# One 128-row DMA per output tile in place of two 64-row DMAs

## Chip, cores and metric

One core of one Trainium2 chip. The metric is the device time of one execution in microseconds (us); medians of several runs are given. A ratio is the mean time of one kernel's runs over that of the other's from the same rounds, so it is not quite the ratio of the medians quoted.

## The reference, cut to what matters

A decayed linear attention in blocks of 64 tokens (4 batches, 8 heads, 768 tokens, head size 64), and then an MLP on its 3072 x 512 output. Only the last line writes memory: 3072 rows of 512 fp32, 6.29 MB.

```python
intra = einsum(einsum(qb, kb) * Dmask, vb)
inter = einsum(qb * lam_pow, kv_state)          # kv_state is carried from block to block
x = attn_out.transpose(0, 2, 1, 3).reshape(B * S, H * D)
h = x @ w_in
g = h + sin(alpha * h) ** 2 / (alpha + 1e-09)
return g @ w_out                                 # [3072, 512] fp32
```

## The kernel before

The work is a list, `ORDER`, of small steps with the engine for each; every engine runs its own steps in the order of the list. Six row groups `g` of 512 tokens have four output tiles `m` of 128 rows each. Unit `u` is a quarter of a row group's attention: loads of q, k, v (`ld`), two DMA transposes (`tdq`, `tdk`), scores on TensorE (`s`), their mask on VectorE (`m`). SyncE (`S`) issues all loads, transposes and stores (`st.g.m.par`).

```python
outp = ctx.enter_context(tc.tile_pool(name="outp", bufs=4))     # four output buffers
# ...
def out_rows(g, m):
    _, tp, b, _, _ = where(4 * g + 2 * (m // 2))
    r0 = b * S + tp * W + (m % 2) * C
    return out[r0:r0 + C].rearrange("(p two) d -> two p d", two=2)

def out_copy(g, m, eng, **_):
    obs[g, m] = outp.tile([P, DM], FP32, name="ob")
    copy(eng, obs[g, m][:], ops.pop((g, m))[:])                 # PSUM to SBUF

def store(g, m, par, **_):
    nc.sync.dma_start(out=out_rows(g, m)[par], in_=obs[g, m][par * D:(par + 1) * D, :])
```

The loads bring two neighbouring tokens to one partition, so the even rows of an output tile lie in partitions 0 to 63 and the odd rows in 64 to 127. That is why the store has a `par` for parity, and why each of its two DMAs writes every second row. The last tile is stored in column pieces by other code, which the change does not touch.

Of the kernel before, what the change touches and what calls it, by code (L numbers as in the profile page):

```python
# [625 lines left out]
```

## Time and profile before

| | |
|---|---|
| median time | 215.98 us when predicted; 216.06 with a fourth run |
| span in the profile | 213.8 us |
| TensorE busy | 204.0 us, 95% |
| DMA engines busy | about 100% up to some 128 us, little after |
| stores of 64 rows | 46, each 64 packets of 2 KB; 20 of them from 185 us on |

The prediction shows the lines. One more is the page's packet count of the kernel before; "under 512 B" counts the 256 B packets of the transposes and the small completion records (4 B) that a DMA leaves.

```profile
DMA packets 64009, 33.92 MB, mean 159 GB/s; under 512 B 19680, under 2 KB 61040, under 8 KB 63984
```

### The profile page before, as it was taken

The numbers are of one execution on the slowest core, as the hardware profiler recorded it, in microseconds if no ns is written. First come the engines' busy times: TensorE is split into PE (matmuls) and PEld (weight loads), VectorE is DVE, ScalarE is ACT, GpSimd is POOL, SyncE is SP. The second block draws the span as 40 slices with busy tenths as digits, with TensorE's granted clock in tenths as the row PEclk, the third lists the DMA queues.
The fourth block names the chain that finished last, engine by engine and source line by source line (L and its number), as shares of the span: only waits on it lengthen the run. The fifth ranks groups of instructions, "written<-read, shape, count | busy, mean of one in ns | idle before, by whom it ended". The sixth has DMA issues, their size and how long they took to land.

```text
span 213.8 us, 5465 instructions
## 1 busy us (share of the span) xinstructions
PE 204.0 (95%) x2104; PEld 110.1 (51%) x2132; DVE 129.8 (61%) x235; ACT 123.5 (58%) x244; POOL 141.4 (66%) x208
## 2 busy tenths in 40 slices
PE   7989999999999999999799999999999999999993
PEld 5767544457744554455444554454454444444463
DVE  3885798159599845778667785626884626441120
ACT  3563984077899839986394496936635659131001
POOL 5488389689797999999898996709841728030000
PEclk9999999999999999999999999999999999999999
DMA  5999999999999999989899997520610000171624
GB/s 144 293 235 196 187 204 271 282 291 289 200 205 202 248 213 289 208 103 199 218 268 133 223 179 198 92 49 0 132 44 3 0 0 0 35 179 35 147 51 98
DMA packets 64009, 33.92 MB, mean 159 GB/s; under 512 B 19680, under 2 KB 61040, under 8 KB 63984
## 3 DMA queue, kind: packets, MB, share of 16 engines
q1 hardware_dynamic: 59568, 29.31, 62.5%
q0 software_dynamic: 4224, 4.19, 12.4%
...
q10 hardware_dynamic: 192, 0.07, 0.2%
q14 instruction: 9, 0.07, 0.1%
HBM read 27.28 MB, written 6.29 MB: 157 GB/s over the span
## 4 chain that ended last, share of the span: by engine, by line
PE 67%; POOL 12%; DMA 10%; issue 3%; ACT 2%; SPq 2%; DVE 2%; POOLq 0%; ACTq 0%
PE ops L525 27%; PE hps L482 24%; DMA w_out_sb<-in_moe_w_out_dram 4%; PE bz L564 3%; DMA QT<-KD 2%; PE okv L460 2%; POOL KD L300 2%; POOL kvbd L425 2%; PE sp L368 2%; PE bz L588 2%; DMA st_v<-in_v_dram 2%; POOL QL L300 2%; POOL kvx L421 2%; PE pt L327 2%; SPq L259 2%
## 5 line engine op out<-in xcount | busy, mean ns | idle before, releaser
L482 PE MATMUL hps<-xt,w_in_sb 128*128 128x512 bf16 (+1 forms) x404 | 86.4, 362 | 0.6 <-issue 0.2
L525 PE MATMUL ops<-w_out_sb,gall 128*128 128x512 bf16 x352 | 83.2, 379 | 2.1 <-issue 1.3
L516 DVE SCALAR_TENSOR_TENSOR gall<-s,r_sb,hps 128x512 bf16<-128x512 bf16 x96 | 68.3, 744 | 23.3 <-POOL s L511 11.7
L502 ACT ACTIVATE s<-hps,alpha_sb 128x512 bf16<-128x512 f32 x96 | 63.2, 688 | 25.7 <-PE hps L482 25.1
L482 PEld LDWEIGHTS <-w_in_sb 128*128 128x128 bf16 x416 | 39.8, 98 | 40.6
L511 POOL TENSOR_TENSOR s<-s 128x512 bf16<-128x512 bf16 x35 | 36.3, 1045 | 36.3 <-ACT s L502 35.6
L525 PEld LDWEIGHTS <-gall 128*128 128x128 bf16 x368 | 34.6, 98 | 39.9 <-issue 0.6
L378 DVE TENSOR_TENSOR ST<-sp,mask 128x512 bf16<-128x512 f32 x48 | 31.9, 684 | 4.4 <-PE sp L368 4.2
L509 ACT ACTIVATE s<-s 128x512 bf16<-128x512 bf16 x51 | 31.6, 634 | 1.0 <-DVE gall L516 0.4
L284 DVE COPY ob<-ops 128x512 f32<-128x512 f32 (+1 forms) x13 | 8.6, 659 | 29.2 <-PE ops L525 23.6
L300 POOL TENSOR_TENSOR QL<-st_q,E 128x512 bf16<-128x512 f32 x23 | 23.9, 1042 | 3.6 <-DVE alpha_sb L574 2.2
L300 POOL TENSOR_TENSOR KD<-st_k,R 128x512 bf16<-128x512 f32 x22 | 22.9, 1042 | 3.5 <-DMA st_k<-in_k_dram 1.8
L425 POOL TENSOR_TENSOR kvbd<-kvx,LBD 128x256 bf16<-128x256 f32 x32 | 19.6, 612 | 2.5
L282 ACT COPY ob<-ops 128x512 f32<-128x512 f32 (+2 forms) x13 | 7.1, 547 | 22.4 <-PE ops L550 12.0
L282 ACT CAST xt<-okv 128x256 bf16<-128x256 f32 x29 | 9.8, 374 | 11.8 <-PE okv L460 11.8
L421 POOL TENSOR_TENSOR kvx<-kva,kvs 128x128 f32<-128x128 f32 x32 | 14.7, 460 | 1.2 <-ACT kva L282 1.0
L284 DVE CAST xt<-okv 128x256 bf16<-128x256 f32 x19 | 7.7, 420 | 11.5 <-PE okv L460 11.5
L282 ACT COPY kva<-kvp 128x128 f32<-128x128 f32 x26 | 6.4, 273 | 9.9 <-PE kvp L400 8.9
L368 PE MATMUL sp<-QT 64*64 64x128 bf16 x384 | 9.9, 219 | 1.3 <-DMA QT<-KD 1.3
L282 ACT COPY QT<-pt 128x512 bf16<-128x512 bf16 x9 | 5.2, 591 | 9.8 <-PE pt L327 9.7
L460 PE MATMUL okv<-ST,VB 64*64 64x128 bf16 x384 | 9.9, 220 | 0.0
L282 ACT CAST VB<-st_v 128x512 bf16<-128x512 f32 x14 | 8.6, 625 | 1.9 <-DMA st_v<-in_v_dram 1.8
...
## 6 DMA issues: line engine op xcount, KB each, us to landing
...
QT<-QL SPq DMA_TRANSPOSE x16, 4.1
QT<-KD SPq DMA_TRANSPOSE x16, 3.4
```

The source lines that it names most:

```text
L282: nc.scalar.copy(out=out, in_=in_)
L284: eng.tensor_copy(out=out, in_=in_)
L300: eng.tensor_tensor(out=t[:], in0=stage[u, j][:].rearrange("p h two e -> p two h e"), in1=tab[:, :, hh * HH:(hh + 1) * HH].unsqueeze(3).to ...
L378: nc.vector.tensor_tensor(out=stm[u][:, hd], in0=sps[u][hd][:], in1=mask[:].unsqueeze(2).to_broadcast([P, 2, 2, P]), op=ALU.mult)
L421: eng.tensor_tensor(out=t[:], in0=x, in1=prev[:], op=ALU.add)
L425: eng.tensor_tensor(out=kvbd[u, c][:], in0=x.unsqueeze(2).to_broadcast([P, 2, 2, D]), in1=LBD[:, 2 * hh:2 * hh + 2, :].unsqueeze(3).to_bro ...
L482: f1mm[g, f] = nc.tensor.matmul(out=hps[g, f][:].rearrange("p (b i) -> p b i", b=2)[:, bs] .rearrange("p b i -> p (b i)"), lhsT=w_in_sb[:, ...
L502: nc.scalar.activation(out=s1[g, f][:], in_=hps[g, f][:], func=ACTF.Sin, scale=alpha_sb[:, f:f + 1])
L509: nc.scalar.activation(out=s2[g, f][:], in_=x[:], func=ACTF.Square)
L511: eng.tensor_tensor(out=s2[g, f][:], in0=x[:], in1=x[:], op=ALU.mult)
L516: nc.vector.scalar_tensor_tensor(out=gall[g][:, f, :], in0=s2.pop((g, f))[:], scalar=r_sb[:, f:f + 1], in1=hps.pop((g, f))[:], op0=ALU.mul ...
L525: nc.tensor.matmul(out=ops[g, m][:], lhsT=gall[g][:, f, m * P:(m + 1) * P], rhs=w_out_sb[:, f, :], start=(f == 0), stop=(f == NFC - 1))
```

## The change

Its intent: half as many store issues on SyncE, and transfers of 256 KB from all 128 partitions in place of 128 KB from 64. In the order, the second store of each tile is dropped and the first stays where it was (most of the diff's other lines are the list wrapped anew).

```diff
-tdq.9:S s.8:T a.8.0:G sk.10:G st.0.0.0:S ld.12.0:S tdk.9:S st.0.0.1:S stt.1.6:V stt.1.7:V sin.1.8:A
+tdq.9:S s.8:T a.8.0:G sk.10:G st.0.0.0:S ld.12.0:S tdk.9:S stt.1.6:V stt.1.7:V sin.1.8:A sqr.1.8:A
 ... (22 more such stores dropped)
-    def store(g, m, par, **_):
-        nc.sync.dma_start(out=out_rows(g, m)[par], in_=obs[g, m][par * D:(par + 1) * D, :])
+    def store(g, m, _i, **_):
+        nc.sync.dma_start(out=out_rows(g, m), in_=obs[g, m][:])
```

More of the change, by code (lines that the diff above doesn't have):

```diff
@@ L51 @@
 sin.1.6:A stt.1.4:V stt.1.5:V sin.1.7:A f1.1.9:T:2 kc.9.0:V sqr.1.6:A f1.1.10:T:7 kc.9.1:A sqr.1.7:A
-tdq.9:S s.8:T a.8.0:G sk.10:G st.0.0.0:S ld.12.0:S tdk.9:S st.0.0.1:S stt.1.6:V stt.1.7:V sin.1.8:A
-sqr.1.8:A sin.1.9:A sin.1.10:A stt.1.8:V m.8.0:V f1.1.11:T:3 f1.1.12:T:0 f1.1.13:T:1 sq.11:G
-tdq.10:S sin.1.11:A f1.1.14:T:4 ld.12.1:S ld.12.2:S ld.13.0:S sqr.1.9:V sqr.1.10:A sqr.1.11:G
-stt.1.9:V stt.1.10:V sin.1.12:A sqr.1.12:G sin.1.13:A stt.1.11:V stt.1.12:V m.8.1:V sk.11:G
-f1.1.15:T:2 cv.10:G sin.1.14:A sqr.1.13:A oi.8:T sin.1.15:A tdk.10:S f2.1.0.0:T:3 sqr.1.14:A sk.12:G
@@ L57 @@
-sq.12:G f2.1.0.1:T f2.1.0.2:T a.9.0:G sqr.1.15:A cv.11:A stt.1.13:V stt.1.14:V stt.1.15:V s.9:T
-o.8:T tdq.11:S ld.13.1:S ld.13.2:S k.10:T:0,1 x.8.0:A x.8.1:A m.9.0:V tdk.11:S f2.1.0.3:T m.9.1:V
-oi.9:T kc.10.0:A st.0.1.0:S ld.14.0:S kc.10.1:A o.9:T cv.12:A x.9.0:A s.10:T k.11:T:2,0 f2.1.1.0:T:1
+tdq.9:S s.8:T a.8.0:G sk.10:G st.0.0.0:S ld.12.0:S tdk.9:S stt.1.6:V stt.1.7:V sin.1.8:A sqr.1.8:A
+sin.1.9:A sin.1.10:A stt.1.8:V m.8.0:V f1.1.11:T:3 f1.1.12:T:0 f1.1.13:T:1 sq.11:G tdq.10:S
+sin.1.11:A f1.1.14:T:4 ld.12.1:S ld.12.2:S ld.13.0:S sqr.1.9:V sqr.1.10:A sqr.1.11:G stt.1.9:V
@@ L60 @@
+stt.1.10:V sin.1.12:A sqr.1.12:G sin.1.13:A stt.1.11:V stt.1.12:V m.8.1:V sk.11:G f1.1.15:T:2
+cv.10:G sin.1.14:A sqr.1.13:A oi.8:T sin.1.15:A tdk.10:S f2.1.0.0:T:3 sqr.1.14:A sk.12:G sq.12:G
+f2.1.0.1:T f2.1.0.2:T a.9.0:G sqr.1.15:A cv.11:A stt.1.13:V stt.1.14:V stt.1.15:V s.9:T o.8:T
+tdq.11:S ld.13.1:S ld.13.2:S k.10:T:0,1 x.8.0:A x.8.1:A m.9.0:V tdk.11:S f2.1.0.3:T m.9.1:V oi.9:T
+kc.10.0:A st.0.1.0:S ld.14.0:S kc.10.1:A o.9:T cv.12:A x.9.0:A s.10:T k.11:T:2,0 f2.1.1.0:T:1
 m.10.0:V a.10.0:G x.9.1:A kc.11.0:A kc.11.1:A m.10.1:V oi.10:T k.12:T:2,0 n.6.0:G n.8.0:G n.9.0:G
@@ L61 @@
 s.11:T o.10:T kc.12.0:V f2.1.1.1:T ld.14.1:S m.11.0:V ld.14.2:S n.10.0:G x.10.0:V m.11.1:V
-f2.1.1.2:T ld.15.0:S st.0.1.1:S ld.15.1:S tdq.12:S ld.15.2:S ld.16.0:S ld.16.1:S ld.16.2:S ld.17.0:S
-oc.1.0:A kc.12.1:A x.10.1:A a.11.0:G sk.13:G cv.13:G oi.11:T o.11:T x.11.0:A sq.13:G f2.1.1.3:T
-sq.14:G oc.1.1:A n.7.0:G x.11.1:V f1.2.0:T:6 sin.2.0:A f1.2.1:T:5 sin.2.1:A sqr.2.0:A stt.2.0:V
-ld.17.1:S st.1.1.0:S a.6.1:G n.6.1:G sk.14:G ld.17.2:S st.0.3.0:S st.0.2.0:S f1.2.2:T:2 sin.2.2:A
-sqr.2.1:A stt.2.1:V f1.2.3:T:7 sin.2.3:A f1.2.4:T:0 f1.2.5:T:3 sin.2.4:A f1.2.6:T:4 f1.2.7:T:5
@@ L67 @@
-sqr.2.2:G stt.2.2:V sqr.2.3:A a.5.1:G stt.2.3:V sin.2.5:A f1.2.8:T:6 f1.2.9:T:7 f1.2.10:T:1 sq.15:G
-sk.15:G sqr.2.4:A sin.2.6:A sqr.2.5:A stt.2.4:V f2.1.2.0:T:0 stt.2.5:V cv.14:G f1.2.11:T:3 tdk.12:S
-f1.2.12:T:2 sin.2.7:A f2.1.2.1:T st.0.2.1:S sin.2.8:A sqr.2.6:G sqr.2.7:A stt.2.6:V sin.2.9:A
-stt.2.7:V sqr.2.8:G sin.2.10:A n.11.0:G stt.2.8:V sqr.2.9:A sqr.2.10:A stt.2.9:V stt.2.10:V sq.16:G
-sin.2.11:A sqr.2.11:A tdq.13:S n.5.1:G tdk.13:S tdq.14:S st.0.3.1:S tdk.14:S a.7.1:G a.12.0:G s.12:T
@@ L72 @@
-k.13:T:6,7 kc.13.0:A sin.2.12:A kc.13.1:A sqr.2.12:A m.12.0:V m.12.1:V tdq.15:S f1.2.13:T:1
-f2.1.2.2:T sin.2.13:A sqr.2.13:A oi.12:T s.13:T o.12:T stt.2.11:V f2.1.2.3:T a.13.0:G m.13.0:V
-stt.2.12:V m.13.1:V stt.2.13:V x.12.0:A x.12.1:A f2.1.3.0:T:3 n.13.0:G n.7.1:G a.8.1:G oi.13:T
-sk.16:G oc.1.2:A f1.2.14:T:2 o.13:T k.14:T:1,0 s.14:T sin.2.14:A x.13.0:V x.13.1:V m.14.0:V n.8.1:G
-sq.17:G n.12.0:G kc.14.0:A f2.1.3.1:T m.14.1:V f2.1.3.2:T sqr.2.14:A a.14.0:G kc.14.1:A tdk.15:S
-ld.18.0:S ld.18.1:S oi.14:T ld.18.2:S sq.18:G cv.15:A cv.16:G cv.17:A k.15:T:1,0 o.14:T s.15:T
@@ L78 @@
-tdq.16:S tdk.16:S stt.2.14:V kc.15.0:V x.14.0:V x.14.1:A f1.2.15:T:2 f2.1.3.3:T st.1.2.0:S a.15.0:G
-m.15.0:V kc.15.1:V oi.15:T m.15.1:V ld.19.0:S ld.19.1:S ld.19.2:S s.16:T ld.20.0:S st.1.0.0:S o.15:T
-x.15.0:V k.16:T:1 x.15.1:V sin.2.15:A sqr.2.15:A m.16.0:V oc.1.3:V stt.2.15:V a.11.1:G f2.2.0.0:T:0
-f1.3.0:T:7 kc.16.0:A st.1.0.1:S ld.20.1:S m.16.1:V sin.3.0:A sqr.3.0:A f1.3.1:T:4 f1.3.2:T:6
-sin.3.1:A f1.3.3:T:1 sqr.3.1:A sin.3.2:A sin.3.3:A f1.3.4:T:5 sin.3.4:A f1.3.5:T:2 f1.3.6:T:3
-sk.17:G st.1.2.1:S ld.20.2:S sk.18:G sk.19:G f2.2.0.1:T f2.2.0.2:T a.9.1:G sq.19:G sq.20:G sqr.3.2:G
@@ L84 @@
-stt.3.0:V sqr.3.3:A stt.3.1:V a.16.0:G n.9.1:G sin.3.5:A sqr.3.4:A stt.3.2:V n.14.0:G n.15.0:G
-sin.3.6:A stt.3.3:V stt.3.4:V sqr.3.5:A ld.21.0:S tdq.17:S tdk.17:S sqr.3.6:A cv.18:G tdq.18:S
-tdk.18:S st.1.3.0:S f1.3.7:T:1 oi.16:T stt.3.5:V a.10.1:G s.17:T o.16:T x.16.0:V k.17:T:2 f2.2.0.3:T
-cv.19:G m.17.0:V stt.3.6:V x.16.1:V kc.17.0:A f2.2.1.0:T:2 a.17.0:G n.10.1:G n.11.1:G sk.20:G
-cv.20:G a.12.1:G f2.2.1.1:T tdq.19:S ld.21.1:S tdk.19:S ld.21.2:S ld.22.0:S st.1.1.1:S tdq.20:S
-ld.22.1:S tdk.20:S m.17.1:V oi.17:T oc.2.0:V s.18:T st.1.3.1:S k.18:T:3 k.19:T:0 o.17:T kc.18.0:A
@@ L90 @@
-f2.2.1.2:T a.18.0:G sin.3.7:A x.17.0:A x.17.1:A n.12.1:G f2.2.1.3:T m.18.0:V m.18.1:V f1.3.8:T:3
-oi.18:T oc.2.1:V sqr.3.7:A sin.3.8:A sqr.3.8:A sq.21:G ld.22.2:S ld.23.0:S st.2.1.0:S sk.21:G
-kc.19.0:V s.19:T o.18:T k.20:T:2 kc.20.0:A m.19.0:V stt.3.7:V f1.3.9:T:0 m.19.1:V f1.3.10:T:4
-sin.3.9:A stt.3.8:V a.19.0:G f1.3.11:T:1 st.2.0.0:S x.18.0:A x.18.1:V sqr.3.9:G sk.22:G sin.3.10:A
-sqr.3.10:A f1.3.12:T:3 f1.3.13:T:2 oi.19:T stt.3.9:V sin.3.11:A sqr.3.11:A sin.3.12:A stt.3.10:V
-cv.21:A f2.2.2.0:T:0 f2.2.2.1:T f2.2.2.2:T stt.3.11:V a.20.0:G sqr.3.12:A sin.3.13:A o.19:T s.20:T
@@ L96 @@
-f1.3.14:T:1 x.19.0:A sqr.3.13:G sq.22:G x.19.1:V sin.3.14:A m.20.0:V stt.3.12:V f1.3.15:T:6
-f1.4.0:T:7 sqr.3.14:G stt.3.13:V stt.3.14:V sin.3.15:A sin.4.0:A sqr.3.15:A sqr.4.0:A stt.3.15:V
-stt.4.0:V tdq.21:S st.2.0.1:S ld.23.1:S f2.2.2.3:T oc.2.2:A f1.4.1:T:4 a.13.1:G cv.22:G sin.4.1:A
-sqr.4.1:G m.20.1:V f1.4.2:T:3 f1.4.3:T:0 sin.4.2:A sin.4.3:A sqr.4.2:A sqr.4.3:A sq.23:G
-f2.2.3.0:T:1 f2.2.3.1:T tdk.21:S tdq.22:S ld.23.2:S oi.20:T n.13.1:G f2.2.3.2:T f2.2.3.3:T o.20:T
-k.21:T:2 stt.4.1:V s.21:T stt.4.2:V stt.4.3:V kc.21.0:V oc.2.3:A f2.3.0.0:T:0 f1.4.4:T:3 f2.3.0.1:T
@@ L102 @@
-f1.4.5:T:2 x.20.0:A sin.4.4:A sin.4.5:A sqr.4.4:G a.15.1:G sqr.4.5:G stt.4.4:V m.21.0:V m.21.1:V
-stt.4.5:V f1.4.6:T:1 sin.4.6:A tdk.22:S tdq.23:S sqr.4.6:A stt.4.6:V a.21.0:G st.2.3.0:S f2.3.0.2:T
-f1.4.7:T:6 f1.4.8:T:3 f2.3.0.3:T sk.23:G oc.3.0:V f1.4.9:T:1 f1.4.10:T:5 f1.4.11:T:4 x.20.1:V
-sin.4.7:A sin.4.8:A sqr.4.7:G sqr.4.8:G stt.4.7:V stt.4.8:V cv.23:A f1.4.12:T:2 tdk.23:S st.3.0.0:S
-sin.4.9:A sqr.4.9:A stt.4.9:V sin.4.10:A sqr.4.10:G stt.4.10:V f2.3.1.0:T:3 f2.3.1.1:T n.15.1:G
-sin.4.11:A st.2.2.0:S st.2.1.1:S sqr.4.11:A stt.4.11:V oi.21:T o.21:T k.22:T:0 k.23:T:1 s.22:T
@@ L108 @@
-x.21.0:V m.22.0:V x.21.1:V m.22.1:V f2.3.1.2:T f2.3.1.3:T oc.3.1:V st.2.3.1:S a.14.1:G n.14.1:G
-kc.22.0:A a.22.0:G oi.22:T o.22:T s.23:T m.23.0:V f2.3.2.0:T:0 f2.3.2.1:T x.22.0:V kc.23.0:A
-x.22.1:A m.23.1:V a.23.0:G oi.23:T f2.3.2.2:T f1.4.13:T:3 o.23:T x.23.0:V f1.4.14:T:4 x.23.1:V
-f1.4.15:T:1 sin.4.12:A sqr.4.12:A stt.4.12:V sin.4.13:A st.2.2.1:S st.3.0.1:S sin.4.14:A sqr.4.13:A
+f2.1.1.2:T ld.15.0:S ld.15.1:S tdq.12:S ld.15.2:S ld.16.0:S ld.16.1:S ld.16.2:S ld.17.0:S oc.1.0:A
+kc.12.1:A x.10.1:A a.11.0:G sk.13:G cv.13:G oi.11:T o.11:T x.11.0:A sq.13:G f2.1.1.3:T sq.14:G
@@ new lines @@
+oc.1.1:A n.7.0:G x.11.1:V f1.2.0:T:6 sin.2.0:A f1.2.1:T:5 sin.2.1:A sqr.2.0:A stt.2.0:V ld.17.1:S
+st.1.1.0:S a.6.1:G n.6.1:G sk.14:G ld.17.2:S st.0.3.0:S st.0.2.0:S f1.2.2:T:2 sin.2.2:A sqr.2.1:A
+stt.2.1:V f1.2.3:T:7 sin.2.3:A f1.2.4:T:0 f1.2.5:T:3 sin.2.4:A f1.2.6:T:4 f1.2.7:T:5 sqr.2.2:G
+stt.2.2:V sqr.2.3:A a.5.1:G stt.2.3:V sin.2.5:A f1.2.8:T:6 f1.2.9:T:7 f1.2.10:T:1 sq.15:G sk.15:G
+sqr.2.4:A sin.2.6:A sqr.2.5:A stt.2.4:V f2.1.2.0:T:0 stt.2.5:V cv.14:G f1.2.11:T:3 tdk.12:S
+f1.2.12:T:2 sin.2.7:A f2.1.2.1:T sin.2.8:A sqr.2.6:G sqr.2.7:A stt.2.6:V sin.2.9:A stt.2.7:V
@@ new lines @@
+sqr.2.8:G sin.2.10:A n.11.0:G stt.2.8:V sqr.2.9:A sqr.2.10:A stt.2.9:V stt.2.10:V sq.16:G sin.2.11:A
+sqr.2.11:A tdq.13:S n.5.1:G tdk.13:S tdq.14:S tdk.14:S a.7.1:G a.12.0:G s.12:T k.13:T:6,7 kc.13.0:A
+sin.2.12:A kc.13.1:A sqr.2.12:A m.12.0:V m.12.1:V tdq.15:S f1.2.13:T:1 f2.1.2.2:T sin.2.13:A
+sqr.2.13:A oi.12:T s.13:T o.12:T stt.2.11:V f2.1.2.3:T a.13.0:G m.13.0:V stt.2.12:V m.13.1:V
+stt.2.13:V x.12.0:A x.12.1:A f2.1.3.0:T:3 n.13.0:G n.7.1:G a.8.1:G oi.13:T sk.16:G oc.1.2:A
+f1.2.14:T:2 o.13:T k.14:T:1,0 s.14:T sin.2.14:A x.13.0:V x.13.1:V m.14.0:V n.8.1:G sq.17:G n.12.0:G
@@ new lines @@
+kc.14.0:A f2.1.3.1:T m.14.1:V f2.1.3.2:T sqr.2.14:A a.14.0:G kc.14.1:A tdk.15:S ld.18.0:S ld.18.1:S
+oi.14:T ld.18.2:S sq.18:G cv.15:A cv.16:G cv.17:A k.15:T:1,0 o.14:T s.15:T tdq.16:S tdk.16:S
+stt.2.14:V kc.15.0:V x.14.0:V x.14.1:A f1.2.15:T:2 f2.1.3.3:T st.1.2.0:S a.15.0:G m.15.0:V kc.15.1:V
+oi.15:T m.15.1:V ld.19.0:S ld.19.1:S ld.19.2:S s.16:T ld.20.0:S st.1.0.0:S o.15:T x.15.0:V k.16:T:1
+x.15.1:V sin.2.15:A sqr.2.15:A m.16.0:V oc.1.3:V stt.2.15:V a.11.1:G f2.2.0.0:T:0 f1.3.0:T:7
+kc.16.0:A ld.20.1:S m.16.1:V sin.3.0:A sqr.3.0:A f1.3.1:T:4 f1.3.2:T:6 sin.3.1:A f1.3.3:T:1
@@ new lines @@
+sqr.3.1:A sin.3.2:A sin.3.3:A f1.3.4:T:5 sin.3.4:A f1.3.5:T:2 f1.3.6:T:3 sk.17:G ld.20.2:S sk.18:G
+sk.19:G f2.2.0.1:T f2.2.0.2:T a.9.1:G sq.19:G sq.20:G sqr.3.2:G stt.3.0:V sqr.3.3:A stt.3.1:V
+a.16.0:G n.9.1:G sin.3.5:A sqr.3.4:A stt.3.2:V n.14.0:G n.15.0:G sin.3.6:A stt.3.3:V stt.3.4:V
+sqr.3.5:A ld.21.0:S tdq.17:S tdk.17:S sqr.3.6:A cv.18:G tdq.18:S tdk.18:S st.1.3.0:S f1.3.7:T:1
+oi.16:T stt.3.5:V a.10.1:G s.17:T o.16:T x.16.0:V k.17:T:2 f2.2.0.3:T cv.19:G m.17.0:V stt.3.6:V
+x.16.1:V kc.17.0:A f2.2.1.0:T:2 a.17.0:G n.10.1:G n.11.1:G sk.20:G cv.20:G a.12.1:G f2.2.1.1:T
@@ new lines @@
+tdq.19:S ld.21.1:S tdk.19:S ld.21.2:S ld.22.0:S tdq.20:S ld.22.1:S tdk.20:S m.17.1:V oi.17:T
+oc.2.0:V s.18:T k.18:T:3 k.19:T:0 o.17:T kc.18.0:A f2.2.1.2:T a.18.0:G sin.3.7:A x.17.0:A x.17.1:A
+n.12.1:G f2.2.1.3:T m.18.0:V m.18.1:V f1.3.8:T:3 oi.18:T oc.2.1:V sqr.3.7:A sin.3.8:A sqr.3.8:A
+sq.21:G ld.22.2:S ld.23.0:S st.2.1.0:S sk.21:G kc.19.0:V s.19:T o.18:T k.20:T:2 kc.20.0:A m.19.0:V
+stt.3.7:V f1.3.9:T:0 m.19.1:V f1.3.10:T:4 sin.3.9:A stt.3.8:V a.19.0:G f1.3.11:T:1 st.2.0.0:S
+x.18.0:A x.18.1:V sqr.3.9:G sk.22:G sin.3.10:A sqr.3.10:A f1.3.12:T:3 f1.3.13:T:2 oi.19:T stt.3.9:V
@@ new lines @@
+sin.3.11:A sqr.3.11:A sin.3.12:A stt.3.10:V cv.21:A f2.2.2.0:T:0 f2.2.2.1:T f2.2.2.2:T stt.3.11:V
+a.20.0:G sqr.3.12:A sin.3.13:A o.19:T s.20:T f1.3.14:T:1 x.19.0:A sqr.3.13:G sq.22:G x.19.1:V
+sin.3.14:A m.20.0:V stt.3.12:V f1.3.15:T:6 f1.4.0:T:7 sqr.3.14:G stt.3.13:V stt.3.14:V sin.3.15:A
+sin.4.0:A sqr.3.15:A sqr.4.0:A stt.3.15:V stt.4.0:V tdq.21:S ld.23.1:S f2.2.2.3:T oc.2.2:A
+f1.4.1:T:4 a.13.1:G cv.22:G sin.4.1:A sqr.4.1:G m.20.1:V f1.4.2:T:3 f1.4.3:T:0 sin.4.2:A sin.4.3:A
+sqr.4.2:A sqr.4.3:A sq.23:G f2.2.3.0:T:1 f2.2.3.1:T tdk.21:S tdq.22:S ld.23.2:S oi.20:T n.13.1:G
@@ new lines @@
+f2.2.3.2:T f2.2.3.3:T o.20:T k.21:T:2 stt.4.1:V s.21:T stt.4.2:V stt.4.3:V kc.21.0:V oc.2.3:A
+f2.3.0.0:T:0 f1.4.4:T:3 f2.3.0.1:T f1.4.5:T:2 x.20.0:A sin.4.4:A sin.4.5:A sqr.4.4:G a.15.1:G
+sqr.4.5:G stt.4.4:V m.21.0:V m.21.1:V stt.4.5:V f1.4.6:T:1 sin.4.6:A tdk.22:S tdq.23:S sqr.4.6:A
+stt.4.6:V a.21.0:G st.2.3.0:S f2.3.0.2:T f1.4.7:T:6 f1.4.8:T:3 f2.3.0.3:T sk.23:G oc.3.0:V
+f1.4.9:T:1 f1.4.10:T:5 f1.4.11:T:4 x.20.1:V sin.4.7:A sin.4.8:A sqr.4.7:G sqr.4.8:G stt.4.7:V
+stt.4.8:V cv.23:A f1.4.12:T:2 tdk.23:S st.3.0.0:S sin.4.9:A sqr.4.9:A stt.4.9:V sin.4.10:A
@@ L112 @@
+sqr.4.10:G stt.4.10:V f2.3.1.0:T:3 f2.3.1.1:T n.15.1:G sin.4.11:A st.2.2.0:S sqr.4.11:A stt.4.11:V
+oi.21:T o.21:T k.22:T:0 k.23:T:1 s.22:T x.21.0:V m.22.0:V x.21.1:V m.22.1:V f2.3.1.2:T f2.3.1.3:T
+oc.3.1:V a.14.1:G n.14.1:G kc.22.0:A a.22.0:G oi.22:T o.22:T s.23:T m.23.0:V f2.3.2.0:T:0 f2.3.2.1:T
+x.22.0:V kc.23.0:A x.22.1:A m.23.1:V a.23.0:G oi.23:T f2.3.2.2:T f1.4.13:T:3 o.23:T x.23.0:V
+f1.4.14:T:4 x.23.1:V f1.4.15:T:1 sin.4.12:A sqr.4.12:A stt.4.12:V sin.4.13:A sin.4.14:A sqr.4.13:A
 sqr.4.14:G stt.4.13:V stt.4.14:V f1.5.0:T:5 f1.5.1:T:7 sin.4.15:A sqr.4.15:A sin.5.0:A sin.5.1:A
@@ L119 @@
 f2.4.1.0:T:3 f2.4.1.1:T f2.4.1.2:T oc.4.0:V f1.5.14:T:1 sqr.5.10:G stt.5.10:V sqr.5.11:G sqr.5.12:A
-stt.5.11:V stt.5.12:V st.4.0.0:S st.3.2.0:S st.3.2.1:S st.3.3.0:S st.3.1.0:S st.3.3.1:S f1.5.15:T:7
-sin.5.13:A sin.5.14:A st.3.1.1:S f2.4.1.3:T oc.4.1:V sqr.5.13:A sqr.5.14:G sin.5.15:A stt.5.13:V
-stt.5.14:V f2.4.2.0:T:4 st.4.0.1:S st.4.1.0:S st.4.1.1:S sqr.5.15:G stt.5.15:V f2.4.2.1:T f2.4.2.2:T
-f2.4.2.3:T f2.4.3.0:T:0 f2.4.3.1:T f2.4.3.2:T f2.4.3.3:T f2.5.0.0:T:3 f2.5.0.1:T f2.5.0.2:T oc.4.2:V
-oc.4.3:A st.4.3.0:S st.4.2.0:S st.4.3.1:S st.4.2.1:S f2.5.0.3:T oc.5.0:V st.5.0.0:S st.5.0.1:S
-f2.5.1.0:T:2 f2.5.1.1:T f2.5.1.2:T f2.5.1.3:T f2.5.2.0:T:5 f2.5.2.1:T f2.5.2.2:T oc.5.1:V f2.5.2.3:T
-st.5.1.0:S st.5.1.1:S lt.0:T:3 oc.5.2:V st.5.2.0:S lt.1:T:7 st.5.2.1:S ltc.0:A lt.2:T:5 ltc.1:A
-ltc.2:V
+stt.5.11:V stt.5.12:V st.4.0.0:S st.3.2.0:S st.3.3.0:S st.3.1.0:S f1.5.15:T:7 sin.5.13:A sin.5.14:A
+f2.4.1.3:T oc.4.1:V sqr.5.13:A sqr.5.14:G sin.5.15:A stt.5.13:V stt.5.14:V f2.4.2.0:T:4 st.4.1.0:S
+sqr.5.15:G stt.5.15:V f2.4.2.1:T f2.4.2.2:T f2.4.2.3:T f2.4.3.0:T:0 f2.4.3.1:T f2.4.3.2:T f2.4.3.3:T
+f2.5.0.0:T:3 f2.5.0.1:T f2.5.0.2:T oc.4.2:V oc.4.3:A st.4.3.0:S st.4.2.0:S f2.5.0.3:T oc.5.0:V
+st.5.0.0:S f2.5.1.0:T:2 f2.5.1.1:T f2.5.1.2:T f2.5.1.3:T f2.5.2.0:T:5 f2.5.2.1:T f2.5.2.2:T oc.5.1:V
+f2.5.2.3:T st.5.1.0:S lt.0:T:3 oc.5.2:V st.5.2.0:S lt.1:T:7 ltc.0:A lt.2:T:5 ltc.1:A ltc.2:V
 """
```

## The prediction

> **What bounds the kernel now.** I read the page first: the busy shares, the slices, the chain that ended last.
>
> ```profile
> span 213.8 us, 5465 instructions
> PE 204.0 (95%) x2104; PEld 110.1 (51%) x2132; DVE 129.8 (61%) x235; ACT 123.5 (58%) x244; POOL 141.4 (66%) x208
> ...
> DMA  5999999999999999989899997520610000171624
> ...
> q1 hardware_dynamic: 59568, 29.31, 62.5%
> ...
> PE 67%; POOL 12%; DMA 10%; issue 3%; ACT 2%; SPq 2%; DVE 2%; POOLq 0%; ACTq 0%
> ```
>
> TensorE is busy 95% of the span and holds two thirds of the chain, so the kernel is close to TensorE bound. But the DMA row stands at 9 until about 128 us (slice 24), with single lower digits: in the first 60% there is little room for more DMA work. After that the DMA engines are nearly idle. q1 carries the loads, transposes and stores that SyncE issues.
>
> Next the chain in order of time, for 50 to 125 us. Between 72 and 115 us it leaves TensorE:
>
> ```profile
> 76.78 1.97 SPq L259
> ...
> 79.94 4.26 DMA st_v<-in_v_dram
> ...
> 102.03 2.79 DMA st_k<-in_k_dram
> ...
> 110.00 5.34 DMA QT<-KD
> ...
> 115.38 0.42 PE sp L368 x16
> ```
>
> A load or a transpose that lands later here moves TensorE. From 131 us on the chain is TensorE alone. Last, the stores themselves, in the view of the output tensor, and SyncE's timeline from 150 us:
>
> ```profile
> L540 SPq DMA_DIRECT2D out_dram<-ob x46: 466/588/1743, 58.8 to 208.1; - x46
> ...
> DMA to landing us min/median/max: 1.9/2.6/4.3
> ```
>
> ```profile
> 151.06 57.66 SPq L540 DMA_DIRECT2D out_dram<-ob  x26
> 208.99 2.38 SPq L560 DMA_DIRECT2D out_dram<-ob  x4
> ```
>
> A store costs SyncE 0.59 us and lands 2.6 us after its issue begins. Of the 46, 20 are issued from 185 us to the end: the output of the last row groups leaves in the last 28 us.
>
> **What the Trainium skill says.** (1) "DMA: Bandwidth & Descriptors", Rules for kernel authors, on two transfers to disjoint partition halves: "Don't bother — they serialize"; one 128-partition transfer is to be used. That is the change's intent. (2) The same page, Why a DMA increments its semaphore by 16 and not by 1: the number k of DMA engines is the largest number up to 16 that divides the slowest non-size-1 dimension of both access patterns, as the instruction carries them; and on the SyncE path the lowest-numbered k engines are used. This is the point on which I chose. In the built program the old store writes [64, 512] from 64 partitions: k = 16. The new one writes a view [2, 64, 512], because even and odd rows lie in different halves of the tile, from 128 partitions: k = 2. The trace of before cannot confirm k = 2: its large transfers all have 128 or 64 outermost. (3) The same page, Queues, rings and completion order: each DMA engine consumes its ring in order. So what SyncE issues after a store waits, on those two engines, until the store's packets are through. The trace agrees about the limit of one engine only in this way: 512 B packets take 27 ns in the packet records, which is 19 GB/s an engine and 303 GB/s for 16, and the slices' GB/s never exceed 293.
>
> **The change part by part.**
>
> *Removed:* 23 issues on SyncE, 23 x 0.59 = 13.6 us of its queue. Nine of them fall between 58 and 131 us, where SyncE issues almost without a gap: 9 x 0.63 (with gaps) = 5.7 us. The chain passes through SyncE for only some 3.6 us in that stretch, so the most this can return is about 3 us. No arithmetic changes; the other engines' order is the same.
>
> *Added:* the 128 rows of a store are 128 packets of 2 KB. Over 16 engines the old pair put 2 x 4 on each; on two engines it is 64 on each. A 2 KB packet has a median of 87 ns in the packet records from 58 to 131 us, and 84 at the least (about 154 from 160 us on, where 16 engines read one half of the partitions together; with two engines I choose 84). So a store occupies the two engines for 64 x 84 ns = 5.4 us. Besides, landing takes about 1.5 us (2.6 less the issue and four packets).
>
> *The middle, 58 to 131 us.* I keep a ledger of one of those two engines from the first store at 58.8 us (0.6 us to issue: 59.4). A load is 512 packets of 512 B, 32 on each engine, 32 x 27 ns = 0.86 us; a transpose is 32 x 18 ns (256 B packets) = 0.6 us. Ahead of and with the k transpose of unit 12, SyncE's order has 5 stores (27.0), 18 loads (15.5) and 7 transposes (4.2): 46.7 us. The engine is never idle meanwhile by this ledger, so this transpose is through at 59.4 + 46.7 = 106.1 and lands at 107.6. TensorE needs it here, in its timeline:
>
> ```profile
> 91.86 0.42 PE L368 MATMUL sp<-QT 64*64 64x128 bf16 x16
> ```
>
> That is a stall of 15.7 us, all on the path: TensorE's order is fixed. Onward to the k transpose of unit 19: 3 stores (16.2), 11 loads (9.5), 14 transposes (8.4) end at 140.2 and land at 141.7. Its scores stood at 122.7, now 138.4: 3.2 us more. The later units have more room than backlog. Sum of the middle: +19 us. The saved issues lie inside these waits. Bubbles may add to it: SyncE's waits in the built program show that each DMA waits for the one eight places earlier, so a blocked engine blocks the issue too.
>
> *131 to 185 us.* TensorE alone; the shift stays, and the five stores issued at 151 to 154 us drain (27 us).
>
> *The tail.* The first of the last ten stores goes out at 185.1 us (before the shift), because SyncE's order puts it first and its copy ends then. On the two engines: 185.7 + 10 x 5.4 = 239.7, landing and the small last stores +2: 241.7, against an end at 213.8. That is +28 us. Four output buffers are too few for this backlog. Already before there is one wait for one:
>
> ```profile
> DVE ob L284 <- DMA out_dram<-ob: 2.9, 1, 2.9
> ```
>
> Copies will now wait for stores, and with them TensorE for its banks. Most of it lies within the same 54 us of store work; I add 2 us for moments when the two engines run dry meanwhile.
>
> Sum: span 213.8 + 19 + 28 + 2 = 263, and the measured time is 2.2 us over the span (215.98 against 213.8): 265 us.
>
> **The rivals.**
>
> *The store still uses 16 engines.* For it: 128 partitions on the SBUF side, and rule (1). Against it: rule (2) looks at both sides, and the built program keeps the 2 outermost. Then packets per engine are unchanged, SyncE saves its 13.6 us, the chain perhaps 0 to 3: 213 to 216 us.
>
> *Two engines, but hidden.* Nobody reads the output; stores run beside matmuls. Then only the last store shows, 5 us at the end: about 221 us. Against it: the loads stand behind the stores on the same rings, with the chain passing through a transpose at 110 us, and ten stores at the end are 54 us of work in 28 us of time. That a store is off the chain says nothing when its engine rate falls eightfold.
>
> *Two engines at the slow packet.* If a packet takes 154 ns as at the end of the old kernel, a store takes 9.9 us and the tail alone gives +70 us or more: above 310 us. Against it: the 154 ns appear only where all 16 engines write at once from one half of the partitions; two engines share less.
>
> **Range and chances.** Two engines at 84 ns, with the middle between +8 and +38 and the tail between +22 and +36, gives 246 to 290; I set 243 to 290. The 16-engine rival gets 8%, the hidden one 3%, the slow packet 4%. So slower by over 2%: 0.91; within 2%: 0.07; faster: 0.02.
>
> **What would show each step right or wrong.** Right: stores landing in 7 us or more when nothing stands before them, and in over 15 where they queue; transposes and loads after 60 us landing much later than 4 to 5 us; TensorE idle for some 15 us shortly after 90 us, released by a transpose; copies to the output tile waiting for stores near the end; a last stretch of some 25 us or more with TensorE nearly idle and stores draining at about 2 x 24 GB/s. Wrong: stores still landing in under 4 us, which means 16 engines; a middle without a new TensorE wait, which means that the loads had slack that I don't see; packets of 2 KB well over or under 84 ns, which scales both terms.

## The result, and the profile after

The changed kernel takes 270.64 us (median of 4 runs, 268.83 to 272.27); the ratio to the kernel before is 1.2534 (95% interval 1.2446 to 1.2622). The result of the computation is right.

The page of the changed kernel: span and busy engines, the 40 slices of TensorE, of its granted clock and of DMA, GB/s, the packet count, and the chain by engine.

```profile
span 270.3 us, 5428 instructions
PE 212.3 (79%) x2104; PEld 113.4 (42%) x2132; DVE 129.8 (48%) x235; ACT 124.0 (46%) x244; POOL 141.6 (52%) x208
...
PE   8999999999979900899777997999999999842000
...
PEclk9999999999999975599959999799999999995555
DMA  5999999999979769794859998311000011111121
GB/s 159 293 198 193 224 275 284 287 186 95 270 153 200 199 67 57 114 221 130 168 86 155 182 71 120 88 33 48 30 0 0 4 47 52 51 52 51 51 76 46
DMA packets 63318, 33.90 MB, mean 125 GB/s; under 512 B 18990, under 2 KB 60350, under 8 KB 63294
...
PE 38%; DMA 37%; SPq 7%; POOL 6%; ACT 5%; issue 3%; DVE 1%; POOLq 0%; ACTq 0%; DVEq 0%
```

Three things are to be seen. In the last eight slices the DMA share is a tenth or two and the rate stands at some 51 GB/s: two of 16 engines are writing. TensorE has a hole at slices 14 and 15 (counted from 0; 95 to 108 us), and is idle at the end. And the packets "under 512 B" are 690 fewer. If each of the 46 stores of before ran on 16 engines and left a record for each, they left 46 x 16 = 736; 690 fewer leaves 46, which is 23 x 2. So each of the 23 stores ran on two DMA engines; that this way of counting holds is tested below with other views.

The waits of the changed kernel, the greatest in which a DMA ended the wait (us in all, times, longest; the weight loads ahead of the same matmuls, 21.4 us, are left out):

```profile
DVE ob L281 <- DMA out_dram<-ob: 39.4, 5, 14.7
...
ACT ob L279 <- DMA out_dram<-ob: 26.1, 3, 19.9
...
PE sp L365 <- DMA QT<-KD: 20.2, 5, 14.3
```

The one wait for an output buffer of before, 2.9 us, has become eight with 65.5 us, and TensorE's wait for transposes has gone from 1.3 to 20.2 us. TensorE's timeline shows the longest, at the scores of unit 12, which began at 91.86 us before:

```profile
108.72 0.64 PE L365 MATMUL sp<-QT 64*64 64x128 bf16 x16 [14.29 <-DMA QT<-KD]
```

To divide the 56.5 us by which the span grew, I looked for the same place in both traces before the final stretch: the start of a row of 49 output matmuls, at 188.73 us in the chain before and at 217.77 us in the chain after. What lies up to there in each (us; then TensorE, weight loads, VectorE, ScalarE and GpSimd busy, granted clock, DMA share, GB/s), the kernel before first:

```profile
0.00:188.73 188.73, 182.46 (x1975) 98.65 (x2003) 124.05 (x226) 121.33 (x240) 139.38 (x207) 1.00 0.80 167
```

and the changed kernel:

```profile
0.00:217.77 217.77, 189.66 (x1975) 101.23 (x2002) 124.09 (x226) 121.78 (x240) 139.54 (x207) 0.94 0.79 143
```

The same 1975 matmuls begin this row 29.0 us later: 21.8 us of it are TensorE idle (28.1 against 6.3), 7.2 us are busy time at a lower clock. From there to the end it takes 52.5 us in place of 25.1, which is 27.4 us more. So the loss is 29.0 us in the middle and 27.4 us at the end.

### The profile page after: what moved, and what is told of

The parts are those of the page before. It is cut to its first block, busy times and chain, and to the rows that moved or that the text cites. A ratio compares the mean times of both kernels' runs of the same rounds, so it can differ in the third digit from the quotient of the medians.

```text
span 270.3 us, 5428 instructions
## 1 busy us (share of the span) xinstructions
PE 212.3 (79%) x2104; PEld 113.4 (42%) x2132; DVE 129.8 (48%) x235; ACT 124.0 (46%) x244; POOL 141.6 (52%) x208
## 2 busy tenths in 40 slices
DMA packets 63318, 33.90 MB, mean 125 GB/s; under 512 B 18990, under 2 KB 60350, under 8 KB 63294
## 4 chain that ended last, share of the span: by engine, by line
PE 38%; DMA 37%; SPq 7%; POOL 6%; ACT 5%; issue 3%; DVE 1%; POOLq 0%; ACTq 0%; DVEq 0%
PE ops L522 17%; DMA out_dram<-ob 14%; PE hps L479 14%; DMA QT<-KD 12%; DMA st_k<-in_k_dram 5%; SPq L256 5%; DMA w_out_sb<-in_moe_w_out_dram 3%; ACT s L499 3%; DMA st_v<-in_v_dram 2%; SPq L537 2%; PE sp L365 2%; PE okv L457 2%; POOL s L508 2%; POOL QL L297 1%; POOL kvx L418 1%
## 5 line engine op out<-in xcount | busy, mean ns | idle before, releaser
L479 PE MATMUL hps<-xt,w_in_sb 128*128 128x512 bf16 (+1 forms) x404 | 88.3, 367 | 3.0 <-DVE gall L513 2.2
L522 PE MATMUL ops<-w_out_sb,gall 128*128 128x512 bf16 x352 | 86.0, 388 | 2.6 <-issue 1.7
L513 DVE SCALAR_TENSOR_TENSOR gall<-s,r_sb,hps 128x512 bf16<-128x512 bf16 x96 | 68.2, 742 | 31.3 <-POOL s L508 20.2
L522 PEld LDWEIGHTS <-gall 128*128 128x128 bf16 x368 | 35.3, 100 | 42.6 <-issue 5.1
L365 PE MATMUL sp<-QT 64*64 64x128 bf16 x384 | 10.7, 232 | 20.2 <-DMA QT<-KD 20.2
L418 POOL TENSOR_TENSOR kvx<-kva,kvs 128x128 f32<-128x128 f32 x32 | 14.7, 459 | 18.6 <-ACT kva L279 18.5
L422 POOL TENSOR_TENSOR kvbd<-kvx,LBD 128x256 bf16<-128x256 f32 x32 | 19.6, 612 | 2.5
L365 PEld LDWEIGHTS <-QT 64*64 64x64 bf16 x384 | 7.0, 113 | 23.3 <-DMA QT<-KD 21.4
L281 DVE CAST xt<-okv 128x256 bf16<-128x256 f32 x19 | 7.7, 419 | 12.4 <-PE okv L457 12.4
L547 PE MATMUL ops<-w_out_sb,gall 128*128 128x128 bf16 (+1 forms) x48 | 4.7, 267 | 10.0 <-DVE ob L281 10.0
```

Source lines behind the costliest of these rows:

```text
L365: nc.tensor.matmul(out=sp[hd][half[c], par, hp, :], lhsT=QT[half[hd], 1, par, hp, half[c]], rhs=QT[half[hd], 0, :, hp, half[c]], start=Tru ...
L418: eng.tensor_tensor(out=t[:], in0=x, in1=prev[:], op=ALU.add)
L422: eng.tensor_tensor(out=kvbd[u, c][:], in0=x.unsqueeze(2).to_broadcast([P, 2, 2, D]), in1=LBD[:, 2 * hh:2 * hh + 2, :].unsqueeze(3).to_bro ...
L479: f1mm[g, f] = nc.tensor.matmul(out=hps[g, f][:].rearrange("p (b i) -> p b i", b=2)[:, bs] .rearrange("p b i -> p (b i)"), lhsT=w_in_sb[:, ...
L513: nc.vector.scalar_tensor_tensor(out=gall[g][:, f, :], in0=s2.pop((g, f))[:], scalar=r_sb[:, f:f + 1], in1=hps.pop((g, f))[:], op0=ALU.mul ...
L522: nc.tensor.matmul(out=ops[g, m][:], lhsT=gall[g][:, f, m * P:(m + 1) * P], rhs=w_out_sb[:, f, :], start=(f == 0), stop=(f == NFC - 1))
```

## The experiments

My theory: the output view [2, 64, 512] holds a store to two DMA engines; loads and transposes queue behind it there, and the last ten stores have to drain. The rivals: a 128-row store is slow as such, or merging is; the loss is one store's time and scales with it; the waits for output buffers make the end; the place of the stores, not the work of the two engines, makes the middle; the lower clock makes part of it.

"Shift" is how much later an instruction starts than the same one in the kernel before, in their traces, one of each kernel; for units, it is the first mask of the unit on VectorE, matched by its place among the masks. In the changed kernel it is 17.1 us at unit 12, 22.6 at unit 17, 25.5 at unit 19 and 29.0 at unit 23. Differences of about 1 us say nothing: the run with the change at the end alone executes the same instructions as the kernel before up to 185 us, and its shift goes from -0.6 us at unit 15 to -1.7 at unit 17. A result that is wrong on purpose is only so in the order of output rows.

### Only the outermost dimension of the view: 16, 8 and 4 in place of 2

```diff
-        nc.sync.dma_start(out=out_rows(g, m), in_=obs[g, m][:])
+        nc.sync.dma_start(out=tile_rows(g, m).rearrange("(p q) d -> q p d", q=16), in_=obs[g, m][:])
```

(`tile_rows` is `out[r0:r0 + C]` in memory order; q is 16, 4 and 8.)

> Wrong on purpose: the rows of each tile land in another order. One 128-row store per tile as in the changed kernel, but its output view is [16, 8, 512] instead of [2, 64, 512]; bytes, packets, number and place of the stores are the same. My theory (the outermost 2 of the output view confines a store to 2 DMA engines): 16 engines again, stores land in under 4 us, and the time falls from 270.6 to 212 to 217 us. Rival (a 128-row store is slow as such, because it is one transfer of 256 KB or has a three-dimensional view): stays at 265 to 275 us.

Measured: 214.43 us, ratio 0.9896 (0.9841 to 0.9951), inside the forecast. Nothing but the order of rows within the tile has changed, and the loss of 25% is gone. So a store of 128 rows is not slow; the outermost dimension is what counts.

> Wrong on purpose in the same way, with the view [4, 32, 512]. My theory: 4 engines, 32 packets of 84 ns = 2.7 us of each per store. The ledger of the prediction with 2.7 in place of 5.4 us gives +2 us at the scores of unit 12 and nothing more later; ten last stores are 27 us of work in 28 us of time, so +1 to +2 at the end: 217 to 223 us, far from halfway. Rival (the loss goes as the time that one store takes, so it halves when that halves): 216 + 54.6 / 2 = 243 us. Rival (size or view as such): 270 us.

Measured: 233.95 us, ratio 1.0795. That is outside my forecast of 217 to 223 us, and the halving rival (243) missed too. The trace divides it. At the end, where I expected next to nothing, the shift grows only from 14.7 to 17.4 us: ten stores of 2.7 us do nearly fit. But the middle lost 14.7 us, not 2; there, half of the 29.0 us of the changed kernel, the halving rival was right. The ledger of the middle was too kind.

> Wrong on purpose like the runs with 16 and 4 outermost, with the view [8, 16, 512]. It tests a corrected ledger for the middle. In the kernel before, the packet records from 58 to 131 us already give each DMA engine 74 us of packet time in 73 us (21.5 transposes, 35.1 loads, 10.5 stores, 6.8 completion records), because packets take longer on average than their median, which my prediction used. With k engines a store takes 128 / k x 84 ns: ten stores 54 us (k = 2), 27 (k = 4), 13.4 (k = 8). Theory (sum of mean packet times against 73 us): 63.4 + 27 = 90, an excess of 17 where 14.7 was measured as the shift for k = 4; 63.4 + 13.4 = 77, an excess of 4 for k = 8, so a shift of 1 to 5 us at unit 23 and 216 to 220 us. Rival (the loss is proportional to a store's time on its engines): half of that of k = 4 again, 7 us and 223 to 226 us.

Measured: 217.81 us, ratio 1.0103 (1.0053 to 1.0153), shift 2.4 us at unit 23: as the sum of mean packet times gave, and not 7 us as the proportional rival would have it. The packet counts of the four pages settle the number of engines; in this order, for 16, 8 and 4 outermost:

```profile
DMA packets 63640, 33.91 MB, mean 160 GB/s; under 512 B 19312, under 2 KB 60672, under 8 KB 63616
```

```profile
DMA packets 63456, 33.90 MB, mean 157 GB/s; under 512 B 19128, under 2 KB 60488, under 8 KB 63432
```

```profile
DMA packets 63364, 33.90 MB, mean 147 GB/s; under 512 B 19036, under 2 KB 60396, under 8 KB 63340
```

Each is 19680 - 736 + 23 x k: 19312 for k = 16, 19128 for 8, 19036 for 4, and 18990 for the 2 of the changed kernel.

### Two stores per tile, but each on two engines

```diff
-        nc.sync.dma_start(out=out_rows(g, m)[par], in_=obs[g, m][par * D:(par + 1) * D, :])
+        nc.sync.dma_start(out=out_rows(g, m)[par].rearrange("(p q) d -> q p d", q=2),
+                          in_=obs[g, m][par * D:(par + 1) * D, :])
```

> Wrong on purpose (row order within each half tile). The kernel before, with its two 64-row stores per tile, but each has the output view [2, 32, 512]. Nothing is merged. My theory: 2 engines, 32 packets of 84 ns = 2.7 us for each of 46 stores, the same 64 packets on each of the two engines per tile: as slow as the changed kernel, 262 to 280 us. Rival (the merging of two stores is what costs): 216 us.

Measured: 276.12 us, ratio 1.2737. The kernel before with all its 46 stores, and with nothing merged, is as slow as the changed kernel once its view has 2 outermost (it is even 5 us slower, which stays open). Merging is cleared.

### The two halves of the loss, each alone

```diff
+    def one_store(g, m):
+        return 4 * g + m <= 12        # the other run: > 12
+
     def store(g, m, par, **_):
+        if one_store(g, m):
+            if par == 0:
+                nc.sync.dma_start(out=out_rows(g, m), in_=obs[g, m][:])
+        else:
             nc.sync.dma_start(out=out_rows(g, m)[par], in_=obs[g, m][par * D:(par + 1) * D, :])
```

> Right result. The order and stores of the kernel before, but the 13 tiles stored up to 154 us are stored by one DMA of 128 rows ([2, 64, 512]) as in the changed kernel; the ten tiles stored from 185 us on keep two DMAs of 64 rows. My theory (two separate losses: loads and transposes behind stores in the middle, and the drain of ten stores at the end): the masks of unit 23 shift by 29 us as in the changed kernel, and the end by as much: 243 to 247 us. Rival (one loss feeds on the other, so that they don't add): under 238 us or over 252 us.

> Right result. The counterpart: only the ten tiles stored from 185 us on by one DMA of 128 rows. My theory: nothing shifts before 185 us, and ten stores of 64 x 84 ns on two engines end the kernel 27 us later: 242 to 245 us; with the 29 us of the other part it gives the 54.6 us measured. Rival (the loss at the end is the copies' wait for output buffers that the middle left full): under 235 us.

Measured: 244.57 us (ratio 1.1289) with the change in the middle alone, shift 29.2 us at unit 23 and 29.2 still at the last full tile; 242.95 us (ratio 1.1237) with the change at the end alone, where nothing is late up to 185 us (shift -1.7 us at unit 23). 12.9% and 12.4% make 25.3%, which is the whole. The two losses are separate and add.

### The copies' waits for output buffers taken away

```diff
-        obs[g, m] = outp.tile([P, DM], FP32, name="ob")
+        if 4 * g + m > 12:                      # the last ten tiles: stage buffers, free by then
+            nm = "qkv"[(4 * g + m) % 3]
+            spare = stagep.tile([P, HH, 2, D], FP32, name=f"st_{nm}")
+            obs[g, m] = spare[:].rearrange("p h two e -> p (h two e)")
+        else:
+            obs[g, m] = outp.tile([P, DM], FP32, name="ob")
```

> Right result. The changed kernel, but the last ten tiles take their output buffers from the stage buffers, which are free by then, in place of the pool of four; so no copy waits for a store at the end. It takes away nearly all of the 65 us in which copies wait for stores, the greatest waits of the changed kernel's profile but one. My theory (the two DMA engines have 54 us of stores to write after 214 us whatever the copies do): TensorE ends some 20 us earlier, the kernel not: 267 to 271 us. Rival (the copies' wait for buffers makes the end late): 245 to 255 us.

Measured: 269.74 us, ratio 1.2487, in range. Of the 65.5 us of waits for output buffers, one wait of 1.3 us is left, and the kernel ends when it did. Its timeline from 230 us on:

```profile
234.54 4.95 SPq L542 DMA_DIRECT2D out_dram<-st_q  x1
...
235.81 3.70 PE L552 MATMUL ops<-w_out_sb,gall 128*128 128x256 bf16 x48
...
239.59 5.07 SPq L542 DMA_DIRECT2D out_dram<-st_v  x1
...
244.76 4.93 SPq L542 DMA_DIRECT2D out_dram<-st_q  x1
249.79 5.07 SPq L542 DMA_DIRECT2D out_dram<-st_k  x1
254.95 6.74 SPq L562 DMA_DIRECT2D out_dram<-ob  x4
```

TensorE has done its last matmul at 239.5 us, and 31 us follow in which stores go out, one every 5.0 to 5.2 us. The greatest waits of the changed profile were a symptom of the drain, not a cause of the time.

### Two stores moved away from the transpose that waits

```diff
-st.1.1.0:S a.6.1:G n.6.1:G sk.14:G ld.17.2:S st.0.3.0:S st.0.2.0:S ...
+a.6.1:G n.6.1:G sk.14:G ld.17.2:S st.0.2.0:S ...
-... tdk.13:S tdq.14:S ... tdk.15:S ld.18.0:S
+... tdk.13:S st.0.3.0:S tdq.14:S ... tdk.15:S st.1.1.0:S ld.18.0:S
```

> Right result. The changed kernel with two stores moved in SyncE's order: of the three that stand ahead of the k transpose of unit 12, one goes behind the k transpose of unit 13 and one behind that of unit 15. Nothing else changes, and the two engines have the same work by the transpose of unit 19. Theory A (place in the ring: a transpose waits for the stores just ahead of it): the shift at the mask of unit 12 falls from 17 us to 5 to 9 us, and the time falls below 264 us, because later transposes have more room. Theory B (capacity, the ledger of my prediction: the two engines have more work than the middle has time): the shift at unit 12 falls too, but is back at 22 to 26 us at unit 19, and the time stays at 266 to 272 us. That the run with 4 engines lost half of the middle, where the ledger gave 2 us, speaks for A.

Measured: 270.06 us, ratio 1.2484. The shift at unit 12 falls from 17.1 to 8.8 us, and then climbs to 20.8 at unit 17, 23.6 at unit 19 and 27.3 at unit 23. TensorE's timeline shows one long wait turned into several; the lines are the scores of units 12, 13, 16, 17, 19 and 21:

```profile
100.46 0.64 PE L365 MATMUL sp<-QT 64*64 64x128 bf16 x16 [4.46 <-DMA QT<-KD]
...
106.29 0.64 PE L365 MATMUL sp<-QT 64*64 64x128 bf16 x16 [1.01 <-DMA QT<-KD]
...
119.36 0.42 PE L365 MATMUL sp<-QT 64*64 64x128 bf16 x16 [0.81 <-DMA QT<-KD]
...
135.79 0.64 PE L365 MATMUL sp<-QT 64*64 64x128 bf16 x16 [2.01 <-DMA QT<-KD]
...
146.30 0.42 PE L365 MATMUL sp<-QT 64*64 64x128 bf16 x16 [0.81 <-DMA QT<-KD]
...
167.05 0.42 PE L365 MATMUL sp<-QT 64*64 64x128 bf16 x16 [1.89 <-DMA QT<-KD]
```

Theory B, capacity, is right for two engines: the same work stands before the transpose of unit 19 wherever the stores are, and moving them only moves the wait.

### TensorE kept busy through the long wait

```diff
-... tdk.14:S a.7.1:G a.12.0:G s.12:T
+... tdk.14:S a.7.1:G a.12.0:G w.120:T:s0 s.12:T
```

> Right result. The changed kernel with 120 idle-filling matmuls of 256 columns[...] ahead of the scores of unit 12, within TensorE's wait of 14.3 us for the transpose. Up to a matched matmul, TensorE had 7.2 us more busy time in the changed kernel than in the one before, for the same matmuls, at a granted clock of 0.50 after that wait. Theory (the wait lets the clock drop and this costs about 2.2 us between the masks of units 12 and 13): the clock stays at 1.00 from 108 to 116 us, the rise of the shift from unit 12 to 13 (17.1 to 19.3 us) is gone. Whether the time falls by that 2 us (267 to 269.5) or not (270 to 272) tells if it lies on the path or is absorbed by the next wait for a transfer.

Measured: 273.13 us, ratio 1.2663, outside both forecasts. The mechanism did what was expected: the 120 matmuls start 109 ns apart and fill TensorE from 94.5 to 107.8 us, the granted clock is 1.00 from 108 to 116 us, and the shift stays at 17.3 us from unit 12 to 15 where it had risen to 19.5. But at unit 17 it is 24.0 us (22.6 without the filling), at unit 23 29.9. The gain is absorbed by the next wait for a transfer. So 7.2 us of slower matmuls are in the trace of the changed kernel, but at this wait they did not set the time. The run's median is 2.5 us above the changed kernel's, but they were measured in different batches, and the intervals of the two ratios overlap (1.2597 to 1.2728 and 1.2446 to 1.2622), so I don't call it slower.

### The intent kept, with 16 engines

A right result with one transfer needs the tokens in the order of memory along the partitions. Three places for that were tried; in each, `out_rows` is `out[r0:r0 + C]`, so both sides of the store are [128, 512] (the code of the last tile follows the new order). The first lets the copy to `xt` write with a stride of 2 elements, the second lets TensorE read q's columns with a stride, the third lets the copy read PSUM with a stride:

```diff
+# first
+copy(eng, xt[...].rearrange("p hp (i two) -> p hp two i", two=2),
+     okv[u][c][:, 0:2 * P].rearrange("p (hp two i) -> p hp two i", hp=2, two=2))
+# second, in the scores and inter-block matmuls, with the mask's iota in the same order
+rhs=QT[half[hd], 0, :, hp, half[c]].rearrange("p par i -> p i par"),
+# third
+copy(eng, xt[...].rearrange("p hp (i two) -> p hp i two", two=2),
+     okv[u][c][:, 0:2 * P].rearrange("p (hp two i) -> p hp i two", hp=2, two=2))
```

> Right result. The copies from PSUM to the tile xt put tokens in their order in memory, so that the partitions of an output tile are 128 neighbouring rows, and the store of a tile is one transfer with [128, 512] on both sides. My theory: 16 engines; the output costs nothing more, SyncE saves 23 issues; the 48 copies to xt write with a stride of 2 elements and may take longer than the 374 and 420 ns of before. 212 to 220 us; under 214 if these copies cost nothing. Rival (a 128-row store is slow as such): 265 us and more.

> Right result, and an attempt at a better kernel. The run with strided copies to xt gave the store [128, 512] on both sides but its copies rose from 374 to 449 and from 420 to 442 ns, and the time was that of before. Here TensorE puts the tokens in order: the scores and the inter-block matmuls read the columns of q in the order of memory (a stride in the moving operand), and the mask is built in that order; the copies are as before. If that stride costs TensorE nothing: 213 to 215 us, as the run with 16 outermost (214.4), about 1% under the kernel before. If TensorE reads the strided operand more slowly, these 464 matmuls of 128 columns rise from some 218 ns and the time is above 217 us.

> Right result, the other attempt. As the run with strided copies to xt, but the copy reads PSUM with the stride and writes xt contiguously. If it was the write with a stride of 2 elements that lengthened the copies: their mean falls back to 374 and 420 ns and the time to 213.5 to 215.5 us. If the read costs the same: 215.5 to 218 us.

Measured, all with right results: 216.82 us (ratio 1.0002, 0.9946 to 1.0058), 224.73 us (1.0410) and 215.83 us (0.9998, 0.9953 to 1.0044). The groups of instructions show what each stride costs (busy, mean ns). The first, its copies on ScalarE and VectorE, against 374 and 420 ns before:

```profile
L279 ACT CAST xt<-okv 128x256 bf16<-128x256 f32 x29 | 11.6, 449 | 12.4 <-PE okv L457 10.2 <-PE hps L479 1.9
L281 DVE CAST xt<-okv 128x256 bf16<-128x256 f32 x19 | 8.1, 442 | 12.3 <-PE okv L457 8.5 <-PE hps L479 3.9
```

The second, its 464 strided matmuls at 284 ns against 219 before:

```profile
L365 PE MATMUL sp<-QT 64*64 64x128 bf16 x384 | 16.2, 284 | 0.0
...
L443 PE MATMUL okv<-QT,kvbd 128*128 128x128 bf16 x80 | 13.6, 284 | 0.1
```

The third, whose copies are as short as before:

```profile
L279 ACT CAST xt<-okv 128x256 bf16<-128x256 f32 x29 | 9.8, 374 | 12.5 <-PE okv L457 10.6 <-PE hps L479 1.8
```

The third does all that the change wanted and is no faster than the kernel before. Does the saving in issues reach the end at all? Between units 15 and 17, where SyncE was on the chain before, its shift falls by 1.5 us (from +0.7 to -0.8), and in the run with 16 outermost also by 1.5 (from -0.2 to -1.7). But in the run with the change at the end alone, which saves no issue up to there, it falls by 1.1 us too (from -0.6 to -1.7). So most of this fall belongs to the one traced execution of the kernel before, and at most some 0.4 us of the 13.6 us of saved issues shows. The run with 16 outermost was 1% faster than the kernel before (its interval ends at 0.9951) and the third was not; what makes that difference stays open.

## Why the prediction was right

**Two engines: right, shown.** The completion records count them, and the views with 4, 8, 16 and with two stores on two engines each leave nothing of the rivals "16 engines", "128 rows" and "merging". Which two engines they are no run shows, since the records do not name the engine; that ten queued stores together move 51 GB/s at a DMA share of 0.13 (2 of 16 is 0.125) says that they share the same two.

**A store's time on them: right, slightly too long.** 5.4 us was predicted from 84 ns a packet; issues follow each other at 5.0 to 5.2 us when only stores run, which with the 51 GB/s for two engines is 80 ns a packet. The choice of 84 against 154 ns was right, too: the records from 58 to 131 us of the changed kernel have a median of 84. The slow-packet rival is out, and what was said against it fits the records: for the last ten tiles' stores the median is 154 ns before, when 16 engines read 64 partitions at a time, and 84 and 86 ns in the run with 16 outermost and in the third one with a right result, where 16 engines read all 128.

**The end: right.** +28 and 2 us were predicted, 27.4 measured. It is a drain, and the 2 us for buffers were not needed.

**The middle: right in mechanism, too small.** At unit 12 the ledger gave 15.7 us where 17.1 were measured, and "3.2 us more" up to unit 19, where the shift is 25.5; then "the later units have more room than backlog", where it rises to 29.0. So the +19 of the sum measured 29. (The total, 265 us for 270.6, is closer than this part because the end was put 2.6 us too high.) One reading of SyncE's order was wrong as well: of the five stores that the prediction has issued at 151 to 154 us, two stand ahead of the transposes of unit 21 and a third ahead of the k transpose of unit 23. With the prediction's own packet times this would have added nothing (18.0 us late at unit 21). The term that was mis-sized is the other work on the two engines: 0.6 us for a transpose and 0.86 for a load come from median packets. The mean packets of the kernel before, from 58 to 131 us, are 26.9 ns for the transposes and 30.7 for the loads, so 0.86 and 0.98 us. With these in the same ledger, the k transpose of unit 12 lands 19.6 us after TensorE needed it before, that of unit 19 27.8 us, that of unit 21 29.3 us; their scores are in fact 16.9, 25.5 and 27.5 us late, so this ledger is some 2 us too long at each. It was worked out after the result, and is argued, not shown. What speaks for it is the run with 8 outermost, forecast from mean packets and right, and the moved stores, which changed the first wait and not the sum. It stays open how far the packets on just the two full engines lengthened, since the records do not name the engine. And for 4 engines neither way is exact: the plain sum of work gave 17 us where 14.7 were measured, but for 2 engines the plain sum gives 44 where 29 were measured. Where the engines run dry at times, each burst of stores has its own effect, and I have no rule for it.

**What I had not foreseen:** the granted clock. After some waits it stands at 0.50 for some us, and TensorE's busy time up to the matched place grew by 7.2 us. The Trainium skill, "TensorE: Matmul & The Clock Gate", Part 1, says that the clock is halved after an idle window of about 3.4 us. The trace agrees for the long wait, where TensorE fell idle at 94.4 us, the clock was 0.83 in the window from 96 to 98 us, and 0.50 from 98 us to 114. It differs for a shorter one: after a wait of only 1.96 us, from 132.4 to 134.3 us, the clock was 0.72 from 134 to 136 us and 0.50 from 136 to 140. Keeping TensorE busy through the first wait repaired the clock and not the time.

**SyncE's saved issues:** at most 3 us were granted to them; where 16 engines keep the rest equal, at most some 0.4 us show, which is within what two executions differ by.

## What to carry to other kernels

Before two DMAs are merged, look at the outermost dimension of both access patterns as the program carries them: a merge that puts a 2 in front of 64 rows takes 14 of 16 DMA engines away, and the count of completion records in a profile shows it at once. A store that nobody reads is not free when its engines also serve loads: sum the work per DMA engine, with mean and not median packet times, against the time of each stage. A long list of waits for buffers at the end of a kernel may be only the shadow of a drain; take the waits away before you believe in them.

## What the Trainium skill lacked or had wrong

- The Trainium skill, "DMA: Bandwidth & Descriptors", Rules for kernel authors: the row on transfers to disjoint partition halves advises one 128-partition transfer without a condition. Followed here, with the halves holding alternate rows, it cost 25% (270.64 against 216.06 us); with 16 outermost the same bytes in the same number of transfers took 214.43 us. The row on using all 16 engines in the same table has the condition, but gives leading broadcast dimensions as its example, and the two rows do not refer to each other. What the page says of how k is chosen (Why a DMA increments its semaphore by 16 and not by 1) was confirmed by the completion records for k = 2, 4, 8 and 16.
- The same page, Specifications, gives about 27 GiB/s for an engine (29 GB/s) and no packet time for stores. Measured: 2 KB packets from SBUF to HBM at 80 to 84 ns, so two engines write 51 GB/s and one some 25.6.
- No page says how the cost of narrow transfers goes with the number of their engines: here 8 engines for the stores cost 1%, 4 cost 8%, 2 cost 25%, in a kernel whose DMA engines were busy at 90% or more in nearly all of the first 60% of the span.
- "SBUF — State Buffer", Door 1: The DMA port swizzle, in its note on cachelines, gives 8 bf16 elements as a stride without cost. ScalarE's copies that write bf16 with a stride of 2 elements took 449 ns against 374. Reading PSUM with a stride of 64 fp32 cost the copies nothing (374 ns); bf16 columns 256 elements apart as a matmul's moving operand cost 284 ns against 219, for which no page has a number.
